# Reordering the first batch of a block-sorted attention and its following projections: two-bank tiles for two v mixes, and two pairs' scores in one session

## The chip, the cores and the metric

The kernel runs on one core of a Trainium2 chip. The time is device microseconds (us) of one execution, and a quoted time is a median of several. A profile is one execution's trace. Its *span* runs from the first to the last recorded instruction and is about 2 us shorter than the time. Engines: PE is TensorE, PEld its weight load, DVE VectorE, ACT ScalarE, POOL GpSimd, SP the queue that issues transfers and DMA transposes.

## The reference, cut to what matters

```python
for _ in range(5):                         # P: softmax, then column normalisation, of sort_net
    P = softmax(P); P = P / P.sum(-2)
k_sorted = einsum('bhij,bhjcd->bhicd', P, k_b)   # "mix" of k over 8 blocks of 96 rows
v_sorted = einsum('bhij,bhjcd->bhicd', P, v_b)   # "mix" of v
attn = softmax(scale * q_b @ k_sorted.T)         # per block, 96 x 96
x = (attn @ v_sorted)                            # 4 batches x 768 tokens, 8 heads x 64 -> 512
out = ((x @ w_a) * (x @ w_b)) @ w_out            # 512 -> 1536 -> 512
```

Two heads make a pair; a batch has four. Attention of batch 0 is done in two halves of four blocks, so that projections of its first half can start while the second half's attention goes on. Batch 0's halves are the changed code.

## The kernel before

The buffers in PSUM, and the helpers:

```python
psA = tile_pool(bufs=2, space=PSUM)     # tiles [128, 2, 512] fp32: two banks each
psF = tile_pool(bufs=4, space=PSUM)     # tiles [128, 512] fp32: one bank each

def mix_first(g, what, engines, fill=0, cols=512):   # 12 matmuls, two copies out
    mix = [psF.tile([P, 512], FP32, tag="F") for _ in range(2)]
    keep_busy(mix[0], fill, cols)                    # dummy matmuls
    mix_mms(g, what, lambda c: mix[c // 3][:, c % 3 * P:(c % 3 + 1) * P])
    for u, eng in enumerate(engines):
        copy(eng, turned(g, what, u), mix[u] ...)    # to kT / vT of pair g

def half_scores(h, hp):   # 8 matmuls into a psA tile, ACT exponential -> eT
def half_v(hp):           # 4 transposes of vT into a psF tile, DVE copy -> vs
def second_v(hp):         # the second half's v: a DMA transpose of vT -> vs
def half_o(h, hp):        # 8 matmuls eT x vs into psA; DVE reciprocal and multiply -> xph
def half_x(h, hp, eng):   # 4 transposes of xph into psF, copy by eng -> xT
def partial(n, *kcs):     # projection matmuls of chunks kcs, begun before the last xT chunk
                          # n < 3: psF tile, n = 3, 4: a psA tile ("two")
# ... cut: order of the first half (see the diff)
# ... cut: ffn_ab(b, m, t): 4 w_a and 4 w_b matmuls, ACT copy a_sb, DVE product hT
def c_(g):                # later pairs: turn q, mix k and v, then
    ...
    if g > HP: return_v(g)                           # DMA transpose vT -> vs, by SP
    if g >= 2 * HP - 2:
        nc.gpsimd.tensor_copy(out=gate, in_=kTs[g % HP][0:1, 0:1])
        load_later(g)                                # load pair g + 2, by POOL
```

The queues of PE, POOL and SP, and in the changed part of ACT and DVE too, run in the program's order. The kernel text sets no semaphores; the waits are added when it is built.

The softmax here doesn't subtract the row's maximum and nothing guards it: scores larger than these inputs give would overflow.

## Time and profile before

| what | before |
|---|---|
| time, median of 3 (range) | 241.52 us (241.12 to 241.68) |
| span of the profile | 239.3 us |
| first mix starts | 13.02 us |
| first scores of the second half start | 25.80 us |
| first unit of batch 1 (its q transposes) starts | 42.28 us |

I call the stretches between the last three rows the first half (12.78 us) and the second half (16.48 us), and what follows the tail (197.02 us). The page and the lines that carry the reading are in the prediction below.

### The profile page before, as it was taken

The page shows a single profiled execution, that of the slowest core. Times are in us where ns is not written, and L with a number is a line of the kernel's source. Part 1 is how long each engine was busy: PE and PEld are TensorE (multiplying, and loading weights), DVE is VectorE, ACT ScalarE, POOL GpSimd, SP SyncE. Part 2 cuts the span into 40 slices and gives each one's busy share as a digit, 9 for nine tenths or more (in the row PEclk, how much of TensorE's full clock was granted, in tenths as well). Part 3 has the DMA queues.
Part 4 walks back from the last instruction along what each step waited for, and adds up shares of the span by engine and source line. Part 5 has one row for each costly group of instructions (what it writes and reads, how often), then busy time and mean ns, then how long its engine had stood idle before and what let it go on. Part 6 is the DMA issues. An engine that isn't in the chain of part 4 may idle for free.

```text
span 239.3 us, 5178 instructions
## 1 busy us (share of the span) xinstructions
PE 233.4 (98%) x2075; PEld 138.7 (58%) x2075; DVE 109.6 (46%) x258; ACT 100.7 (42%) x187; POOL 70.4 (29%) x97
## 2 busy tenths in 40 slices
PE   7999999999999999999999999999999999999994
PEld 7776566666644556666554455666545566655442
DVE  6788467546444234466416243644543244434110
ACT  3675652674530266644630366355500234333001
POOL 8777348773400055072520508211000000000000
PEclk9999999999999999999999999999999999999999
DMA  5999999999998489679996899970434300000132
GB/s 76 203 198 195 161 191 201 201 201 190 176 171 201 111 138 161 109 121 190 139 196 128 181 133 176 171 144 20 77 79 123 130 1 3 0 0 3 56 119 88
DMA packets 65703, 30.88 MB, mean 129 GB/s; under 512 B 42512, under 2 KB 62736, under 8 KB 65680
## 3 DMA queue, kind: packets, MB, share of 16 engines
q0 software_dynamic: 20944, 14.16, 42.7%
q1 hardware_dynamic: 44592, 16.33, 35.3%
q8 instruction: 16, 0.26, 0.4%
q10 hardware_dynamic: 144, 0.07, 0.1%
q14 instruction: 7, 0.06, 0.1%
HBM read 28.32 MB, written 6.29 MB: 145 GB/s over the span
## 4 chain that ended last, share of the span: by engine, by line
PE 95%; DVE 3%; ACT 1%; issue 0%; DVEq 0%
PE pf L360 52%; PE po L405 24%; PE o_ps L236 3%; PE sc L330 2%; PE heat L167 2%; PE mix L175 2%; PE mix L301 2%; PE mixf L175 1%; PE po L390 1%; PE sc L197 1%; PE xt_ps L227 1%; PE q_ps L265 1%; PE two L360 1%; DVE xp L242 1%; PE vs_ps L213 0%; DVE o_sb L163 0%
## 5 line engine op out<-in xcount | busy, mean ns | idle before, releaser
L381 DVE TENSOR_TENSOR hT<-a_sb,pf 128x384 bf16<-128x384 bf16 x95 | 52.6, 554 | 72.2 <-PE pf L360 46.7
L360 PE MATMUL pf<-xT,w_a_sb 128*128 128x384 bf16 x380 | 78.0, 326 | 0.0
L360 PE MATMUL pf<-xT,w_b_sb 128*128 128x384 bf16 x380 | 77.4, 326 | 0.0
L380 ACT CAST a_sb<-pf 128x384 bf16<-128x384 f32 x95 | 45.4, 479 | 61.8 <-PE pf L360 37.7
L405 PE MATMUL po<-w_out_sb,hT 128*128 128x512 bf16 x276 | 61.9, 379 | 0.0
L360 PEld LDWEIGHTS <-w_b_sb 128*128 128x128 bf16 x384 | 37.5, 98 | 24.7
L360 PEld LDWEIGHTS <-w_a_sb 128*128 128x128 bf16 x384 | 35.2, 98 | 22.7
L405 PEld LDWEIGHTS <-hT 128*128 128x128 bf16 x276 | 26.4, 98 | 30.1
L161 ACT COPY o_sb<-po 128x512 f32<-128x512 f32 (+1 forms) x13 | 7.5, 578 | 48.9 <-PE po L405 47.5
L163 DVE COPY o_sb<-po 128x512 f32<-128x512 f32 (+1 forms) x12 | 7.9, 658 | 38.7 <-PE po L405 34.1
L335 ACT ACTIVATE eT<-sc 96x768 bf16<-96x768 f32 x24 | 18.1, 803 | 5.2 <-PE sc L330 5.2
L242 DVE TENSOR_TENSOR xp<-o_ps,rec 96x512 bf16<-96x512 f32 x24 | 15.9, 684 | 0.3
L317 POOL COPY kT<-turned 128x768 bf16<-128x768 bf16 x6 | 5.0, 831 | 32.5 <-DMA turned<-nat 32.5
L96 POOL DMA_DIRECT2D k<-in_k_dram x16 | 11.6, 724 | 4.9 <-DMA w_a_sb<-in_moe_w_a_dram 1.9
L96 POOL DMA_DIRECT2D v<-in_v_dram x16 | 11.5, 722 | 3.6 <-DMA w_b_sb<-in_moe_w_b_dram 2.4
L236 PEld LDWEIGHTS <-eT 96*128 96x128 bf16 x256 | 10.2, 97 | 3.6 <-DVE xp L242 0.6
L236 PE MATMUL o_ps<-vs,eT 96*128 96x65 bf16 x256 | 11.4, 193 | 0.4 <-DVE vs L214 0.2
L96 POOL DMA_DIRECT2D q<-in_q_dram x12 | 8.7, 723 | 3.5 <-DMA w_a_sb<-in_moe_w_a_dram 2.6
L251 POOL COPY qc<-q 128x768 bf16<-128x768 bf16 x10 | 8.4, 844 | 3.9 <-DMA q<-in_q_dram 3.9
L161 ACT CAST nat<-mix 128x768 bf16<-128x768 f32 (+1 forms) x12 | 7.7, 639 | 4.2 <-PE mix L301 2.5
L167 PE MATMUL heat<-warm 128*128 128x128 bf16 x84 | 8.0, 273 | 1.3 <-DVE warm L77 1.3
L585 POOL COPY gate<-kT 1x1 bf16<-1x1 bf16 x4 | 0.7, 178 | 27.1 <-ACT kT L283 22.6
(86 smaller groups left out, 160.4 us busy)
## 6 DMA issues: line engine op xcount, KB each, us to landing
out_dram<-o_sb SPq DMA_DIRECT2D x17, 256.0 KB, 2.0
k<-in_k_dram POOLq DMA_DIRECT2D x16, 192.0 KB, 5.9
v<-in_v_dram POOLq DMA_DIRECT2D x16, 192.0 KB, 6.6
q<-in_q_dram POOLq DMA_DIRECT2D x12, 192.0 KB, 6.8
w_a_sb<-in_moe_w_a_dram POOLq DMA_DIRECT2D x6, 256.0 KB, 10.1
w_b_sb<-in_moe_w_b_dram POOLq DMA_DIRECT2D x6, 256.0 KB, 11.0
w_out_sb<-in_moe_w_out_dram POOLq DMA_DIRECT2D x3, 512.0 KB, 11.2
out_dram<-o_sb SPq DMA_DIRECT2D x12, 128.0 KB, 2.4
```

The source lines that it names most:

```text
L96: nc.gpsimd.dma_start(out=to, in_=_ap(t, base, [[W, P], [S * D, 2], [1, W]]))
L161: nc.scalar.copy(out=out, in_=in_)
L163: nc.vector.tensor_copy(out=out, in_=in_)
L167: nc.tensor.matmul(ps[:, 0:cols], lhsT=warm[:, 0:P], rhs=warm[:, 0:cols], start=True, stop=True)
L236: nc.tensor.matmul(o_ps[:, e, i * (D + 1):(i + 1) * (D + 1)], lhsT=eT[:, hf, e, i * BLK:i * BLK + P], rhs=vs[0:BLK, i0 + i, V0 - 1 + e * ( ...
L242: nc.vector.tensor_tensor(out=_ap(xp, i0 * 2 * D, [[nxp * 2 * D, BLK], [D, 2], [2 * D, NBH], [1, D]]), in0=_ap(o_ps, 1, [[1024, BLK], [511 ...
L251: nc.gpsimd.tensor_copy(out=qc.rearrange("p c e d -> p e c d"), in_=loaded[g][2].rearrange("p e (c d) -> p e c d", c=NCH))
L335: nc.scalar.activation(out=eT[:, hf, :, 0:HB], in_=sc[0:BLK, :, 0:HB], func=AF.Exp, scale=float(scale))
L360: nc.tensor.matmul(pf[:, 0:HW], lhsT=w_sb[:, kc, m * P:(m + 1) * P], rhs=x_cols(b, kc, t), start=(kc == 0), stop=(kc == KA - 1))
L380: nc.scalar.copy(out=a_sb, in_=pf[:, 0:HW])
L381: nc.vector.tensor_mul(out=hT[:, m, t * HW:(t + 1) * HW], in0=a_sb, in1=ab[1][:, 0:HW])
L405: nc.tensor.matmul(held["po"], lhsT=hTs[b][:, m, c * P:(c + 1) * P], rhs=w_out_sb[:, m, :], start=(m == 0), stop=(m == KO - 1))
```

## The change

Its intent is to take waits and session switches out of TensorE's queue in batch 0. The first half gets a searched order, with the v mixes of pairs 0 and 2 in two-bank tiles to free one-bank buffers. In the second half, scores of two pairs follow each other in one session.

```diff
+    def mix_first(g, what, engines, wide=False, fill=0):
+        if wide:
+            both = psA.tile([P, 2, 512], FP32, tag="A", name="mixa")
+            mix = [both[:, 0], both[:, 1]]
+        else: ...
-            mix_first(0, "v", ("act", "dve"), 2, 256)
-            mix_first(0, "k", ("dve", "act"))
-            mix_first(1, "v", ("act", "dve"), 1)
-            mix_first(1, "k", ("act", "dve"))
+            mix_first(0, "k", ("act", "dve"), fill=2)
+            mix_first(0, "v", ("act", "dve"), wide=True)
+            mix_first(1, "k", ("dve", "act"))
+            mix_first(1, "v", ("act", "dve"))
             half_scores(0, 0)
             half_v(0)
-            mix_first(2, "v", ("act", "dve"))
+            mix_first(2, "v", ("dve", "act"), wide=True)
             mix_first(2, "k", ("act", "act"))
             half_o(0, 0)
+            half_v(1)
             half_scores(0, 1)
-            half_v(1)
             half_v(2)
 # ... cut: xT copies of pairs 0, 2, 3 to ACT and of pair 1 to DVE; half_scores(0, 3), half_v(3) earlier;
 # ... cut: mix_first(3, "k") with its two engines swapped; partial order 0, 2, 1, 0, 3, 4 (was 0, 4, 2, 0, 3, 1)
-            # second half: S0 | S1 | O0 S2 | X0 | O1 S3 | X1 | O2 | X2 O3 | X3
+            # second half: S0 S1 | O0 | O1 X0 | S2 S3 | X1 | O2 | O3 X2 | X3
```

The last two lines sum up the new unit list and its counts: S is half_scores, O half_o, X half_x, and a bar is one projection step or more.

More of the change, by code (lines that the diff above doesn't have):

```diff
@@ L176, in mix_mms @@
                                  rhs=s_all[:, 2 * g + e], start=True, stop=True)
-    def mix_first(g, what, engines, fill=0, cols=512):
-        mix = [psF.tile([P, 512], FP32, tag="F", name="mixf") for _ in range(2)]
-        keep_busy(mix[0], fill, cols)
+    def mix_first(g, what, engines, wide=False, fill=0):
+        if wide:
+            both = psA.tile([P, 2, 512], FP32, tag="A", name="mixa")
+            mix = [both[:, 0], both[:, 1]]
+        else:
+            mix = [psF.tile([P, 512], FP32, tag="F", name="mixf") for _ in range(2)]
+        keep_busy(mix[0], fill, 256)
         mix_mms(g, what, lambda c: mix[c // 3][:, c % 3 * P:(c % 3 + 1) * P])
@@ L183, in mix_first @@
             copy(eng, turned(g, what, u),
-                 _ap(mix[u], 0, [[512, P], [P, 3], [CG, NB], [1, CG]]))
+                 _ap(mix[u], 0, [[1024 if wide else 512, P], [P, 3], [CG, NB], [1, CG]]))
     def turned(g, what, u):
@@ L500, in partial @@
                 ab_mms(begun[n], (w_a_sb, w_b_sb)[n % 2], 0, n // 2, 0, kcs)
-            mix_first(0, "v", ("act", "dve"), 2, 256)
-            mix_first(0, "k", ("dve", "act"))
-            mix_first(1, "v", ("act", "dve"), 1)
-            mix_first(1, "k", ("act", "dve"))
+            mix_first(0, "k", ("act", "dve"), fill=2)
+            mix_first(0, "v", ("act", "dve"), wide=True)
+            mix_first(1, "k", ("dve", "act"))
+            mix_first(1, "v", ("act", "dve"))
             half_scores(0, 0)
             half_v(0)
-            mix_first(2, "v", ("act", "dve"))
+            mix_first(2, "v", ("dve", "act"), wide=True)
             mix_first(2, "k", ("act", "act"))
             half_o(0, 0)
+            half_v(1)
             half_scores(0, 1)
-            half_v(1)
             half_v(2)
-            mix_first(3, "k", ("dve", "act"))
+            mix_first(3, "k", ("act", "dve"))
             half_scores(0, 2)
@@ L518 @@
             mix_first(3, "v", ("act", "act"))
-            half_x(0, 0, "dve")
+            half_x(0, 0, "act")
             half_o(0, 2)
             second_v(1)
-            half_x(0, 1, "act")
             half_scores(0, 3)
+            half_x(0, 1, "dve")
+            half_v(3)
+            half_x(0, 2, "act")
             partial(0, 0)
-            half_v(3)
             partial(0, 1)
-            half_x(0, 2, "dve")
             half_o(0, 3)
             second_v(2)
-            partial(4, 0, 1, 2)
-            partial(2, 0, 1, 2)
-            partial(0, 2)
-            half_x(0, 3, "dve")
-            partial(3, 0, 1, 2)
-            partial(1, 0, 1, 2)
+            partial(2, 0, 1, 2)
+            partial(1, 0, 1, 2)
+            partial(0, 2)
+            half_x(0, 3, "act")
+            partial(3, 0, 1, 2)
+            partial(4, 0, 1, 2)
             begun = [begun[n] for n in range(5)]
@@ L557, in O, with S, X @@
                     second_v(HP - 1)
-            us = [lambda: half_scores(1, 0)]
-            for hp in range(HP):
-                if hp + 1 < HP:
-                    us.append(lambda hp=hp: half_scores(1, hp + 1))
-                if hp > 0:
-                    us.append(lambda hp=hp: half_x(1, hp - 1, "dve"))
-                us.append(lambda hp=hp: O(hp))
-            us.append(lambda: half_x(1, HP - 1, "dve"))
-            return us
+            def S(hp):
+                half_scores(1, hp)
+                half_scores(1, hp + 1)
+            def X(hp):
+                half_x(1, hp, "dve")
+            return [lambda: S(0), lambda: O(0), lambda: O(1), lambda: X(0), lambda: S(2),
+                    lambda: X(1), lambda: O(2), lambda: O(3), lambda: X(2), lambda: X(3)]
         def c_(g):
@@ L657 @@
         steps += [lambda m=m: ffn_ab(0, m, 0) for m in range(3, KO)]
-        interleave(steps, units_half(), (0, 0, 1, 1, 2, 1, 2, 1, 1, 2, 1, 0))
+        interleave(steps, units_half(), (0, 0, 1, 0, 1, 2, 1, 1, 1, 2, 1, 0))
         for b in range(B):
```

## The prediction

> **What bounds the kernel now.** I read the page first, then the chain of work that ended last in order of time, then the timeline from 12 us to 48 us engine by engine, and last the DMA issues of POOL over the same stretch.
>
> ```profile
> PE 233.4 (98%) x2075; PEld 138.7 (58%) x2075; DVE 109.6 (46%) x258; ACT 100.7 (42%) x187; POOL 70.4 (29%) x97
> PE 95%; DVE 3%; ACT 1%; issue 0%; DVEq 0%
> ```
>
> The chain is TensorE for 95% of the span; the DVE 3% is mostly the normalisation loop before 12 us, which the diff doesn't touch. So a microsecond counts only if it leaves TensorE's queue, either as work, as a switch between kinds of work, or as a wait. The 98% cannot be taken as useful time: waits hide in it. The changed code occupies 13.0 us (first mix) to 42.3 us (first unit of batch 1). Everything before is untouched and everything after should only shift.
>
> In the first half (13.0 to 24.1 us) the visible losses are few:
>
> ```profile
> 13.02 0.53 PE L175 MATMUL mixf<-s_all,v 128*64 128x128 bf16 x12 [0.19 <-DVE s_all L153]
> 13.35 0.53 PE L175 MATMUL mixf<-s_all,k 128*64 128x128 bf16 x12
> 13.94 0.38 PE L167 MATMUL mixf<-warm 128*128 128x512 bf16 x1
> 14.25 0.53 PE L175 MATMUL mixf<-s_all,v 128*64 128x128 bf16 x12
> ...
> 21.55 0.42 PE L236 MATMUL o_ps<-vs,eT 96*128 96x65 bf16 x8 [0.18 <-DVE vs L214]
> ```
>
> Read starts, not durations: each group's printed end overlaps the next start. The third mix starts at 14.25, not at about 13.7, because all four one-bank buffers are taken by the first two mixes and a dummy matmul of 512 columns sits in the gap. The last half_o of the phase starts at 21.55 although the transpose before it started at 21.03 and such a group takes about 0.25: it waits about 0.27 us for DVE's copy of v (21.07 + 0.42) and ScalarE's exponential (20.68 + 0.81 = 21.49). Both helpers are nearly without gaps before that. That makes the phase a three-engine race, not a TensorE one.
>
> In the second half (24.1 to 42.3 us) the chain shows what a session of scores costs between projection matmuls:
>
> ```profile
> 25.80 0.35 PE sc L197 x8
> 26.14 1.41 PE pf L360 x8
> 27.55 0.28 PE sc L197 x8
> 27.82 1.41 PE pf L360 x8
> 29.23 0.25 PE o_ps L236 x8
> 29.48 0.28 PE sc L197 x8
> 29.75 1.41 PE pf L360 x8
> 31.16 0.17 PE xt_ps L227 x4
> 31.33 1.30 PE pf L360 x8
> ...
> 59.46 0.45 PE sc L330 x16
> 59.90 1.41 PE pf L360 x8
> ```
>
> Eight projection matmuls take 1.30 us after an output or a transpose session, 1.41 beside a score session: the switch costs 0.11 us on top of 0.28 us of score work, some 0.38 a session (0.35 to 0.38 by starts). One session of 16, as later batches have it, costs 0.45 + 0.11 = 0.56.
>
> **What the skill says.** The Trainium skill, "TensorEngine Tiling (Array Packing)", section Tiling Modes, Key Properties: changing the tiling mode drains TensorE. The trace agrees: scores are 64*128 tiles between 128*128 matmuls, and they show the extra 0.11 us. Outputs and transposes (96*128) show none, so I charge nothing for moving those. "Perfetto Trace Analysis", section Per-engine timelines: a TensorE end time is modelled. Hence I use starts. "PSUM — Partial Sum Buffer", Terms: a bank is 2 KiB per partition and there are eight; the trace's program uses four one-bank and two two-bank buffers, all eight, so a mix in a two-bank tile relieves one pool only by loading the other. No run here shows the collision the same entry warns of.
>
> **The change, part by part.** The first half keeps the same mixes, scores, outputs and partial projections. It drops the 512-column dummy (0.31 us by starts, 13.94 to 14.25), puts k before v, mixes v of pairs 0 and 2 in two-bank tiles, and gives two of the transposed-output copies net to ScalarE. I walked the new order by hand, queue by queue, with durations from the rows (mix 0.33 to 0.45, scores 0.28, half_v 0.32, half_o 0.25 to 0.35, transposes 0.17 to 0.27, ScalarE copy 0.39 to 0.48, exponential 0.71 to 0.81, DVE copy 0.48 to 0.55, reciprocal and multiply 0.92, DVE copies of half_v and xT about 0.4 and 0.3). This is an estimate.
>
> - The four first mixes go out 13.02, 13.37, 13.70, 14.03. The fourth waits a little for the first one's copies (14.14) and ends near 14.4; before it ended at 15.04. That is 0.6 us ahead.
> - The first half_v then needs a one-bank buffer, and with rotation it gets the one DVE empties third: 13.58 + 2 x 0.48 + 0.55 = 15.09. So it starts near 15.1 instead of 15.32: two thirds of the lead is lost at once.
> - First half_o 16.2 (was 16.52), second scores 16.87 (was 16.87; it needs the two-bank tile of the v mix, free at about 16.5, and comes after half_v(1)), second half_o 18.2 (was 18.43), third 19.27 (was 19.51; needs the third exponential, 18.35 + 0.81), fourth scores 19.66 (was 20.20; they now come before a transpose).
> - The last exponential ends near 21.0 instead of 21.49, because ScalarE copies one xT first. DVE copies xT(1) before half_v(3): 20.0 + 0.69 for the third multiply, then 0.3, then 0.42, ends near 21.3. The last half_o starts near 21.36, 0.19 ahead. Three partial sessions fill the wait for its multiply, so the first closing projection matmul starts near 23.9 instead of 24.14. **First half: minus 0.24 us.**
>
> Second half. Four score sessions become two. By the numbers above each merge saves 2 x 0.375 - 0.56 = 0.19 us, 0.38 in all. But the first merged session pays a new wait. The two-bank buffers go round in turn; with partial(4) now after partial(3), the first scores inherit the buffer of partial 3, emptied by the second DVE product of the projections, no longer the one emptied by a ScalarE copy at 25.75. Before, that product ended at 26.03, which is 1.89 us after the first closing matmul at 24.14. TensorE, with nine matmuls of 0.163 us, is ready 1.56 us after it. The wait is 1.94 - 1.56 = 0.38 against 0.10 us before, 0.28 more. Against that, two waits of transposes for the DVE multiply (starts 37.59 and 39.40, some 0.17 and 0.08 us later than a normal follow-on) should go, since an output session or a projection step now stands between: 0.25. **Second half: 0.38 - 0.28 + 0.25 = minus 0.35 us.**
>
> Sum: 0.24 + 0.35 = 0.59 us, 241.52 - 0.59 = 240.93, rounded to 240.9.
>
> **Rivals.** First, weight arrival becomes the wall. POOL's issues show when earlier loads landed, since it stalls for them:
>
> ```profile
> 31.54 0.71 POOL L96 DMA_DIRECT2D k<-in_k_dram  x1 [1.37 <-DMA w_b_sb<-in_moe_w_b_dram]
> 31.82 0.81 PE L360 MATMUL pf<-xT,w_b_sb 128*128 128x384 bf16 x4
> ```
>
> Counting issues and landings in order, that load is the fourth w_b chunk, and the matmuls that use it start 0.28 us later. In my walk these now start at 31.82 - 0.24 + 0.09 (first merge less its wait) - 0.37 + 0.25 (one score session later, one output session earlier) = 31.55, just at the landing. So if the first half gains more than I think, the surplus is taken here: this caps the total near 0.6 us, unless the loads land earlier too. For: DMA moves some 200 GB/s without pause here. Against: transposes by DMA share the engines, and may shift.
>
> Second, the helpers give back all of the first half: if DVE or ScalarE runs as late as before at the last half_o, the gain there is 0, and the total 0.35, 241.2 us. For: both are almost always busy between 13.4 and 21.5. Against: before, ScalarE has gaps of 0.26 and 0.19 us, DVE of 0.21, 0.21 and 0.24, which an order can close; with all closed the last half_o could start near 20.8, a gain of 0.7 us, 240.4 without the weight wall.
>
> Third, the merged sessions stall ScalarE: two exponentials in a row (1.5 us) delay the next projection copy by about 0.65 us and could hold TensorE for a one-bank buffer. The later batches do just that at 51.33 and TensorE shows no wait, so I give it little: 241.5 at worst.
>
> **Range and chances.** The span of the three old runs is 0.56 us, as large as the effect. I add that to a step error of some 0.3 us either way: 240.2 to 241.7. A 2% move is 4.8 us, a fifth of everything between 13 and 42 us that isn't projection work plus more; nothing in the diff adds or removes that. Faster 0.01, within 0.98, slower 0.01.
>
> **What would show it right or wrong.** In the changed trace: fourth mix over by 14.4; last half_o near 21.36; first closing projection matmul near 23.9; first scores of the second half held for a DVE product; two score sessions of 16 at 0.45 us; no wait for xph in the last two transposes; first unit of batch 1 at about 41.7 instead of 42.27, and from there the same distance to the end. The number is wrong if w_b arrives later and TensorE waits for DMA, if buffers don't rotate as assumed, or if a later stage absorbs the shift.

## The result, and the profile after

| | before | after |
|---|---|---|
| time, median of 6 | 241.56 us (240.93 to 242.09) | 240.64 us (240.58 to 240.69, and one slow run of 247.53) |
| ratio of fast runs | | 0.9965, 95% interval 0.9947 to 0.9982 |
| span of the profile | 239.3 us | 238.8 us |
| time less span, profiled run | 241.44 - 239.3 = 2.1 us | 240.58 - 238.8 = 1.8 us |
| first mix starts | 13.02 us | 12.66 us |
| first half | 12.78 us | 13.07 us |
| second half | 16.48 us | 16.01 us |
| tail | 197.02 us | 197.06 us |

A ratio here is the mean time of one kernel's fast runs over that of the other's fast runs of the same rounds, so it isn't quite the ratio of the medians. The small gain is clear of the noise in these runs, and the time falls inside the predicted range. But the table already says that one of the two halves went the wrong way.

The page of the changed kernel, busy time by engine and the chain by engine:

```profile
PE 232.2 (97%) x2074; PEld 138.1 (58%) x2074; DVE 108.9 (46%) x256; ACT 101.4 (42%) x189; POOL 70.4 (29%) x97
PE 92%; DVE 5%; ACT 1%; DMA 1%; issue 1%; DVEq 0%
```

TensorE has 3 points less of the chain and DVE 2 more. Only part of that is the first half, where the path runs through copies of DVE and ACT from 13.55 to 16.86 us and before ran through TensorE almost alone. The rest is the start, no part of the change: up to 5.0 us the path of this profile runs through a load and the normalisation loop, that of the profile before through dummy matmuls. TensorE's timeline of the changed kernel's first half:

```profile
13.66 0.53 PE L175 MATMUL mixf<-s_all,v 128*64 128x128 bf16 x12
14.12 0.34 PE L201 MATMUL sc<-qT,kT 64*128 64x96 bf16 x8
14.68 0.40 PE L217 MATMUL vs_ps<-ident,vT 128*128 128x128 bf16 x4 [0.21 <-DVE vT L163]
...
16.18 0.39 PE L217 MATMUL vs_ps<-ident,vT 128*128 128x128 bf16 x4
16.91 0.35 PE L201 MATMUL sc<-qT,kT 64*128 64x96 bf16 x8 [0.34 <-ACT vT L161]
...
21.49 0.41 PE L240 MATMUL o_ps<-vs,eT 96*128 96x65 bf16 x8
```

The four first mixes come as close together as hoped: the fourth starts 1.00 us after the first, at 13.66. The trouble is the second scores at 16.91. They need a two-bank tile, and it was held by the v mix of pair 2 until ACT had copied it. That group starts 4.25 us after the first mix, against 3.85 in the old order (16.87 - 13.02). So a lead of 0.6 us at the fourth mix (14.61 - 13.02 = 1.59 us before, 1.00 now) has become a lag of 0.40 us. The two lines of before:

```profile
14.61 0.50 PE L175 MATMUL mixf<-s_all,k 128*64 128x128 bf16 x12
16.87 0.34 PE L197 MATMUL sc<-qT,kT 64*128 64x96 bf16 x8
```

Why ACT was late is in its own timeline and in DVE's of the changed kernel:

```profile
15.80 0.55 DVE L163 CAST vT<-mixa 128x384 bf16<-128x384 f32 x1
```

```profile
14.67 0.83 ACT L206 ACTIVATE eT<-sc 96x768 bf16<-96x768 f32 x1
16.38 0.48 ACT L161 CAST vT<-mixa 128x384 bf16<-128x384 f32 x1 [0.88 <-DVE vT L163]
```

DVE copies one bank of the tile from 15.80 to 16.35. ACT, idle since about 15.5, starts on the other bank only at 16.38, 0.03 us after DVE is done. The two banks are different, yet the copies run one after the other. The trace puts ACT's idle time down to DVE's copy, which had ended just before; copies out of two one-bank tiles overlap (v2_narrow, below). The mix of pair 0 shows the same thing turned round: ACT at 13.55, DVE at 14.06 rather than beside it.

TensorE's timeline of the second half, the same kernel:

```profile
25.73 0.64 PE L201 MATMUL sc<-qT,kT 64*128 64x96 bf16 x16
26.30 0.82 PE L364 MATMUL pf<-xT,w_a_sb 128*128 128x384 bf16 x4
...
32.27 0.51 PE L201 MATMUL sc<-qT,kT 64*128 64x96 bf16 x16
32.72 0.82 PE L364 MATMUL pf<-xT,w_a_sb 128*128 128x384 bf16 x4
```

There are now two score sessions of 16. By starts, the second costs 0.45 us, as in the later batches. The first takes 0.57: its second pair waits for the buffer that DVE's second product empties (that product ends at 25.97). Eight projection matmuls after a session still take 1.41 us. So the merge took out two switches, and the second half is 0.47 us shorter.

### The profile page after: what moved, and what is told of

Same layout as the page of the kernel before. It is cut to its first block, busy times and chain, and to the rows that moved or that the text cites. A ratio compares the mean times of both kernels' runs of the same rounds, so it can differ in the third digit from the quotient of the medians.

```text
span 238.8 us, 5175 instructions
## 1 busy us (share of the span) xinstructions
PE 232.2 (97%) x2074; PEld 138.1 (58%) x2074; DVE 108.9 (46%) x256; ACT 101.4 (42%) x189; POOL 70.4 (29%) x97
## 4 chain that ended last, share of the span: by engine, by line
PE 92%; DVE 5%; ACT 1%; DMA 1%; issue 1%; DVEq 0%
PE pf L364 52%; PE po L409 25%; PE o_ps L240 3%; PE sc L334 2%; PE mix L175 2%; PE mix L305 2%; PE po L394 1%; PE sc L201 1%; DMA p_nat<-in_sort_net_dram 1%; PE xt_ps L231 1%; DVE vT L163 1%; PE mixf L175 1%; PE heat L167 1%; PE q_ps L269 1%; PE two L364 1%; DVE xp L246 1%
## 5 line engine op out<-in xcount | busy, mean ns | idle before, releaser
L96 POOL DMA_DIRECT2D k<-in_k_dram x16 | 11.6, 724 | 5.0 <-DMA w_a_sb<-in_moe_w_a_dram 2.0
L240 PEld LDWEIGHTS <-eT 96*128 96x128 bf16 x256 | 10.4, 97 | 3.8 <-DVE xp L246 0.6
## 6 DMA issues: line engine op xcount, KB each, us to landing
w_a_sb<-in_moe_w_a_dram POOLq DMA_DIRECT2D x6, 256.0 KB, 10.4
```

The source lines that it names most:

```text
L96: nc.gpsimd.dma_start(out=to, in_=_ap(t, base, [[W, P], [S * D, 2], [1, W]]))
L240: nc.tensor.matmul(o_ps[:, e, i * (D + 1):(i + 1) * (D + 1)], lhsT=eT[:, hf, e, i * BLK:i * BLK + P], rhs=vs[0:BLK, i0 + i, V0 - 1 + e * ( ...
```

## The experiments

Twelve runs in three sessions, each session on another chip, each kernel beside before on its own chip. "First half" is always the distance from the first mix to the first scores of the second half.

### Which half, and why: second_only, first_only, v2_narrow, before_again

**second_only** is before with the new unit list and counts alone:

```diff
 # before, first half untouched
-            us = [S0 | S1 | O0 S2 | X0 | O1 S3 | X1 | O2 | X2 O3 | X3]
+            us = [S0 S1 | O0 | O1 X0 | S2 S3 | X1 | O2 | O3 X2 | X3]
```

> The kernel before with only the second half's new order (scores of two pairs in one session). Theory A (the gain is the second half's, the first half's new order gives nothing or loses): first closing projection matmul 11.1 us after the first mix as before, second half (from there to the first q transposes of batch 1) about 17.7 us against 18.13 before, time 0.4 to 0.6 us under before, so ratio about 0.998. Rival B (both halves gain): ratio about 0.9985, and the changed kernel clearly faster than this one by 0.3 us or more.

Measured: first half 12.78 us, second half 16.04 us, both as theory A says. The time was not: 243.68 us median, ratio 1.0068 (1.0036 to 1.01), with four fast runs from 241.87 to 243.98 and two slow ones (246.52 and 251.16, clock 0.984 and 0.978). The profile, of a fast run, shows where it went. TensorE's timeline of second_only:

```profile
69.25 1.46 PE L405 MATMUL po<-w_out_sb,hT 128*128 128x512 bf16 x6
72.78 0.65 PE L236 MATMUL o_ps<-vs,eT 96*128 96x65 bf16 x16 [2.07 <-DMA vs<-vT]
```

TensorE stood 2.07 us for the DMA transpose of pair 7's v. And here are busy times and TensorE's granted clock in stretches of 2 us of the same run (after the engines come PEclk, DMA share, GB/s):

```profile
72.00:74.00 2.00, 1.22 (x20) 0.90 (x21) 0.75 (x2) 0.00 (x0) 0.00 (x0) 1.00 1.10 282
74.00:76.00 2.00, 1.78 (x6) 0.73 (x6) 0.95 (x3) 0.59 (x1) 0.00 (x0) 0.52 0.75 215
76.00:78.00 2.00, 2.00 (x7) 0.68 (x7) 0.00 (x0) 0.00 (x0) 0.00 (x0) 0.63 0.73 145
78.00:80.00 2.00, 2.00 (x11) 0.94 (x10) 0.69 (x1) 0.00 (x0) 0.00 (x0) 1.00 0.36 84
```

The wait costs twice: after it the granted clock is 0.52, then 0.63, for some 4 us, and full only by 78 us. The tail is 200.65 us instead of 197.0, so 3.6 us are lost to a wait of 2.07. The lost clock of the two stretches, 2 x 0.48 + 2 x 0.37 = 1.7 us by estimate, accounts for the rest. On this chip, a faster second half alone made the kernel slower. That was no part of theory A or of rival B.

**first_only** is the changed kernel with the old unit list and counts.

> The changed kernel with the second half's old order. Theory A: first closing matmul 11.4 us after the first mix (0.3 us later than before), second half 18.0 to 18.2 us, time equal to before or up to 0.3 us over: ratio 1.000 to 1.0015. Rival B: ratio 0.998 or 0.9985.

Measured: 241.19 us, ratio 1.0013 (0.9979 to 1.0047), fast runs 240.85 to 241.22 apart from the profiled one of 243.23, and one slow run of 246.83. Second half 16.49 us, so the old length. The profiled run is a poor sample for the first half: TensorE waited in it for loads of v (0.3 and 0.9 us), and the first half took 14.35 us. It also waited 0.92 us for the transpose of pair 7's v, until 74.07 us, with no fall of the clock after it, and its tail is 197.81 us. So this run supports theory A by its time and second half only; the rest of the evidence has to come from the next one.

**v2_narrow** is the changed kernel with one word out:

```diff
-            mix_first(2, "v", ("dve", "act"), wide=True)
+            mix_first(2, "v", ("dve", "act"))
```

> The changed kernel with the v mix of pair 2 back in two one-bank tiles. Theory A says the two copies out of one two-bank tile run one after the other (DVE 15.80 to 16.35, then ScalarE 16.38 to 16.86) and hold the second scores until 16.91. Then here both copies overlap, the second scores start 0.3 to 0.5 us earlier after the first mix (4.25 us now, about 3.85 then), and the first closing matmul comes about 11.0 to 11.2 us after the first mix in place of 11.4. Rival: one-bank buffers run short instead (v2 waits for the copies of k1 and v1) and the phase is as long or longer.

Measured: first half 12.74 us, 0.33 less than the changed kernel. The copies overlap again, as ACT's and DVE's timelines of v2_narrow show:

```profile
15.91 0.48 ACT L161 CAST vT<-mixf 128x384 bf16<-128x384 f32 x1
```

```profile
16.13 0.54 DVE L163 CAST vT<-mixf 128x384 bf16<-128x384 f32 x1
```

The second scores start 4.15 us after the first mix (4.25 in the changed kernel); that is less than expected, since k of pair 2 now waits for a one-bank buffer (the rival's point), and the rest is won behind it, as ACT is free earlier. The edit also frees a two-bank buffer, so the 0.33 us is what the order of the copies and the buffer that they hold cost together; no run here separates the two. The time: fast runs 240.56, 240.58 and 241.37, ratio 0.9987 (0.996 to 1.0013), but three of six runs slow (244.8 to 246.3, clock 0.985 to 0.992). Theory A's account of the first half holds in the trace.

**before_again**, a second profile of before:

> The kernel before, unchanged, for a second profile. Theory: the first mix started at 13.02 us in the one profile of before and at 12.66 in that of the changed kernel though no instruction ahead of it differs; that is scatter of the start, so this profile may show either, while first mix to first closing matmul stays at 11.1 us and the second half at 18.1 us. Rival: 13.0 again, which would tie the start to the program.

Measured: 241.68 us for one run, state unknown; first mix at 13.25 us, first half 12.78, second half 16.48, tail 197.09. Over all 14 profiles the first mix starts anywhere from 12.42 to 13.25 us, with either first half. The 0.36 us that the changed kernel's profile gained before the first mix is scatter.

### A wall of transfers: second_delay, second_gate, v2_gate, after_again

**second_delay** adds work to second_only:

```diff
-            mix_first(1, "v", ("act", "dve"), 1)
+            mix_first(1, "v", ("act", "dve"), 3)      # two more dummy matmuls
```

> The kernel with only the second half's new order, plus two more dummy matmuls of 512 columns on TensorE ahead of the third mix, some 0.43 us of pure delay. Theory C (a wall of transfers: that kernel lost time because TensorE, about 1 us ahead, reached the last outputs of batch 0's second half before the transposed v of pair 7 had landed, waited 2.07 us at 70.7 us and then ran several us at a lower granted clock): the added delay removes most or all of the wait, and the kernel with MORE work is faster: fast runs about 240.6 to 241.2 against 241.9 to 244.0 without. Rival D (the long runs were chance, or a fault of the new order itself): 0.4 us slower than without, 242 to 244.

Measured: first half 13.22 us (0.44 longer), tail 197.08, no wait for the transpose, all six runs fast, 240.80 to 241.53, ratio 1.0008 (0.9994 to 1.0022). More work, and steadily faster than second_only. The chips differ, which is why second_only was run once more below.

**second_gate** and **v2_gate** change what the next load waits for, in second_only and in v2_narrow:

```diff
-  nc.gpsimd.tensor_copy(out=gate, in_=kTs[g % HP][0:1, 0:1])
+  nc.gpsimd.tensor_copy(out=gate, in_=vss[g % NBUF][0:1, 0, V0:V0 + 1] if g == 2 * HP - 1
+                        else kTs[g % HP][0:1, 0:1])
```

> The kernel with only the second half's new order, with the load of the pair after pair 8 held until the transposed v of pair 7 has landed (it was held only for pair 7's k copy[...]). Theory C: the transpose lands earlier, no wait for it at 70.7 us, and with the start scatter of 12.4 to 13.2 us the fast runs are 240.2 to 241.0, the new order's 0.46 us at last visible against before (ratio about 0.998). Rival D: no change, 242 to 244.

Measured for second_gate: first half 12.78, second half 16.01 us, and no wait for the transpose in its profile though TensorE came to the outputs at 70.51 us, when second_only's TensorE had to wait. Fast runs 240.81 to 241.29, ratio 1.0006 (0.9991 to 1.0022), so the expected 0.998 was missed, and two of six runs were slow (244.0 and 244.9 us of span). So the hold doesn't remove every loss. The tail of its profile is 0.44 us longer than v2_gate's (197.49 to 197.05); most of that is a wait of 0.34 us, ending at 93.67 us, for a later DMA transpose, of q.

> The changed kernel with pair 2's v mix back in one-bank tiles and the same hold on the load. Theory C: 0.33 us shorter in the first half than the changed kernel, and without the risk of running into the late transpose: fast runs 239.9 to 240.6, ratio 0.997, no slow runs at a clock of 0.99. Rival D: 240.6 at best, slow runs as often as before (3 of 6).

Measured for v2_gate: 240.36 us, all five runs fast, 240.20 to 240.58, ratio 0.9974 (0.9961 to 0.9986). First half 12.74, second 16.01, tail 197.05. POOL's timeline of v2_gate bounds the landing time of the transpose, since POOL waits for it:

```profile
69.60 0.18 POOL L589 COPY gate<-vs 1x1 bf16<-1x1 bf16 x1 [12.12 <-DMA vs<-vT]
```

The transpose had landed by 69.6 us, 1.25 us before the outputs that read it (70.85). Without the hold, second_only's reached TensorE at 72.78. This is the best version and faster than before. That its fast runs beat those of the changed kernel isn't shown: on the same chip two of the latter took 240.40 us (next run); what it has ahead is that none of its five runs was slow, against three of six.

> The changed kernel once more, on this chip, against the same runs of before. Theory: first mix to first scores of the second half 13.07 us, from there to the first q transposes 16.0 us, the end 197.05 us after those, as in its first profile; 240.6 us, ratio 0.9965 to 0.999, about 1.75 us of time outside the span against 2.1 for before. Rival: the ratio of the first session was that chip's and here the two are equal.

Measured for after_again: first half 13.08, second half 16.01, tail 197.02 us, as in the first session. Fast runs 240.40, 240.40 and 241.36, ratio 0.9987 (0.9965 to 1.0009), and three of six runs slow (246.2 to 250.9, clock 0.985 to 0.993), where two of eleven of before were slow. On this chip, then, the change itself isn't clearly faster. Its profile is at the edge: the last outputs are one group at 70.98 us, right after the projections, with no wait shown.

One reading of the traces tells what the wall is. A DMA view of a window with nothing but this transpose's issue gives its time from issue to landing, here of second_only and of v2_narrow:

```profile
vs<-vT SPq DMA_TRANSPOSE x1, 10.4
vs<-vT SPq DMA_TRANSPOSE x1, 5.2
```

| profiles | issued at, us | issue to landing, us | wait of TensorE, us |
|---|---|---|---|
| second_only, second_again, both_narrow | 62.22, 62.38, 62.02 | 10.4, 11.6, 11.8 | 2.07, 3.21, 3.45 |
| first_only | 64.65 | 9.3 | 0.92 |
| before, before_again, before_xact, second_delay | 63.24 to 63.48 | 5.0, 8.2, 5.0, 5.4 | none |
| after, after_again, v2_narrow | 62.54 to 62.71 | 6.2, 8.3, 5.2 | none |
| with the hold: second_gate, v2_gate, after_gate | 62.18 to 62.60 | 7.3, 6.9, 4.3 | none |

In all 14 profiles TensorE is ready for the outputs 8.3 us after the issue, since the issue moves ahead with TensorE. So, other than theory C has it, a lead by itself doesn't use up any slack: the profiles that show a wait are those whose transpose takes clearly over 8.3 us. In those four it lands within about 0.2 us of the q load issued just after it, in the other profiles without the hold 1.5 us or more before that load. The earliest issues without the hold took longest, and second_gate's, as early but with the load held back, took 7.3 us; that speaks for the load as the cause. But before_again's 8.2 us shows the old kernel near the edge too, and why first_only's late issue was slow as well stays open.

### Controls: after_gate, second_again, both_narrow, before_xact

> The changed kernel with only the hold on the load (the pair after pair 8 waits until the transposed v of pair 7 has landed). Theory C (its slow runs, 3 of 6 on the last chip, come from TensorE running into that late transpose): fast runs 240.2 to 240.6 as without the hold, no or one slow run in six. Rival D (slow runs are the chip's own): two to three slow runs again. First half 13.07 us to the first scores of the second half, as without the hold.

Measured for after_gate (the changed kernel with the hold): 240.53 us, none of six runs slow (240.34 to 241.81), ratio 0.998 (0.9963 to 0.9997), first half 13.07. Three slow runs against none in six fits theory C, but the chips differ and no slow run of the changed kernel was profiled, so I don't call their cause shown.

> The kernel with only the second half's new order once more, on another chip than its first session, since the delayed and the held version ran on another chip than it did. Theory C: fast runs again scattered from 240.8 to 244 with slow ones among them, above before on the same chip (ratio 1.002 to 1.007). Rival D: 240.8 to 241.3 and as steady as before, which would make the first session's loss that chip's.

Measured for second_again: two fast runs, 240.58 and 240.95, ratio of those 0.9981, and four of six runs slow (244.56 to 246.85), while all eleven of before on this chip lie between 240.91 and 241.67. The expected ratio above 1 was missed, because here the lost runs are classed as slow. The profiled run, a slow one, has TensorE waiting 3.2 us for the same transpose. The unsteadiness came back on a second chip, so it isn't one chip's.

**both_narrow** is the changed kernel without any two-bank mix.

> The changed kernel with neither v mix in a two-bank tile: what the two-bank tile is worth for pair 0. With pair 0's v in a two-bank tile alone the first scores of the second half come 12.74 us after the first mix. Theory: without it the third mix waits for the first copies as in before (0.3 to 0.5 us), but the copies of v of pair 0 overlap (no 0.29 us hold on DVE), so 12.6 to 13.0. Rival: the two-bank tile is what the new order lives from, and this takes 13.2 us or more.

Measured: first half 12.58 us, the shortest of all, 0.49 below the changed kernel. So in the first half the two-bank tiles cost, both of them, and the new order is better without. But the time of this single run was 244.52 us, state unknown. TensorE's and its weight loads' timelines of both_narrow:

```profile
73.96 1.04 PE L240 MATMUL o_ps<-vs,eT 96*128 96x65 bf16 x16 [3.45 <-DMA vs<-vT]
```

```profile
30.80 0.47 PEld L364 LDWEIGHTS <-w_b_sb 128*128 128x128 bf16 x4 [0.18 <-DMA w_b_sb<-in_moe_w_b_dram]
```

It ran into the wall: 3.45 us, and a tail of 201.6. The second line is the weight arrival that the prediction named: at 30.8 us, earlier than in any other profile, the weight load sat 0.18 us for w_b. In second_only, at 31.02 us, it sat 0.24 us; that fits a second half of 16.04 us there in place of 16.01.

> The kernel before with three of the first half's transposed-output copies on ScalarE and one on DVE, as in the changed kernel (it was one and three): a look at the time outside the span, 2.1 us for all kernels with the old first half and 1.75 with the new one. If the instruction counts of ScalarE and DVE set it, this shows 1.75. If it is 2.1, something else in the first half does, and that stays open. First half within 0.2 us of 12.78.

Measured for before_xact (before with its xT copies moved between ACT and DVE as in the change): 242.15 us for one run, span 240.4, state unknown, so 1.75 us outside the span, as expected if the two engines' instruction counts set it. The span itself holds a wait of 0.71 us, ending at 95.35 us, for the transpose of q that second_gate waited for, so the time says nothing of what the moved copies are worth. First half 12.91 us, 0.13 longer. All kernels with ACT's 189 and DVE's 256 instructions have about 1.75 to 1.8 us outside the span, all with 187 and 258 about 2.1. What happens there isn't recorded, so the mechanism stays open.

## Why the prediction was right or wrong

The time, 240.64 us for 240.9 predicted, is right, and partly by luck. Of the 0.59 us that the two halves were to give, they gave 0.18; a term outside both, which the prediction didn't have, made up for most of the rest. The sign "first unit of batch 1 at about 41.7" came true (41.74) only because this profile's first mix came 0.36 us earlier.

- **Second half, predicted minus 0.35, measured minus 0.47.** The merge of sessions is as predicted. Sized wrong was the new wait ahead of the first merged session: 0.38 us was claimed, "the first scores inherit the buffer of partial 3". They started 1.66 us after the first closing matmul in both kernels (24.07 to 25.73, and 24.14 to 25.80). The start follows ACT's copy of partial 4 (25.18 + 0.50 = 25.68 us), not DVE's product, so the buffers don't go round in turn as I assumed. Only the session's second pair waited for the product, 0.12 us. Of the two transpose waits that were to go (0.25), the later one kept about 0.1 us: pair 3's transposes start 0.26 us after the matmul ahead of them (38.61 to 38.87), as a normal follow-on would 0.16. These terms sum to 0.38 - 0.12 + 0.15 = 0.41 us; the last 0.06 I haven't placed.
- **First half, predicted minus 0.24, measured plus 0.29.** The step that failed is the walk's "it needs the two-bank tile of the v mix, free at about 16.5". On the profile of before's clock (0.36 us later) it came free at 17.2 (16.86 + 0.36). I had let ACT and DVE empty a two-bank tile side by side; then it would have been free when DVE was done, at 16.7 (16.35 + 0.36). The other 0.5 us is ACT's copy, which waited for DVE's. v2_narrow shows what the tile of pair 2 cost, 0.33 us, and both_narrow both tiles, 0.49, of the 0.53 us between prediction and measurement. A smaller slip: the walk's own terms for DVE before the last half_o, 20.0 + 0.69 + 0.3 + 0.42, give 21.4, not "near 21.3". The old profile held the answer, in later batches' v mixes, which use such tiles. DVE, then ACT, of before:

```profile
49.65 0.56 DVE L163 CAST vT<-mix 128x384 bf16<-128x384 f32 x1
```

```profile
50.24 0.48 ACT L161 CAST vT<-mix 128x384 bf16<-128x384 f32 x1
```

ACT begins 0.03 us after DVE ends. There it costs TensorE nothing, which is why I passed over it.

- **What made up for it** lies outside both halves. Time outside the span fell by 0.35 us with the first half's new order, a term that the prediction didn't have. 0.47 - 0.29 + 0.35 = 0.53 us is the repeatable gain; after_gate on its chip had 0.2% of 241 us, about 0.5. The first session's ratio (0.35%, about 0.84 us) is 0.3 us more. Luck of the start, which in the two profiles was 0.36 us, would explain that, but the starts of the other runs aren't known.
- **The first rival, weights as a wall**, named the right kind of limit at the wrong place. Its landing time was read a little late, too. Two lines of the changed kernel, POOL's and TensorE's, show the matmuls on that chunk begin before POOL gets its go:

```profile
31.60 0.71 POOL L96 DMA_DIRECT2D k<-in_k_dram  x1 [1.38 <-DMA w_b_sb<-in_moe_w_b_dram]
```

```profile
31.52 0.81 PE L364 MATMUL pf<-xT,w_b_sb 128*128 128x384 bf16 x4
```

  The w_b chunk was late by little (0.18 us in both_narrow's weight loads, 0.24 in second_only's) and never cost much. The transfer that bites is the DMA transpose of pair 7's v at 70 us: from 40 to 72 us the DMA engines of before move 190 GB/s on average with short pauses, and the transpose took 5.0 us in some profiles and 9.3 to 11.8 in others, against 8.3 us until it is needed. The prediction wrote of transposes that they "may shift" and assumed everything after 42.3 us would only shift; second_only disproves that. That the changed kernel's slower first half spared it most of this is argued from both_narrow, whose faster one met the wall in its single run.
- **The second rival** (helpers give all of the first half back) was nearer the truth than my main line, by another mechanism. **The third** (two exponentials in a row hold TensorE) did not happen: no wait stands in the second half beyond those named.

On the skill: the page "PSUM — Partial Sum Buffer", section PSUM bank collisions raise a hardware error, says that two engines on different banks run clean. By that page the chip would have allowed what I assumed. The trace shows only that one copy waits for the other; that the wait comes from the build and not from the chip isn't shown, as no run here tried the copies without it. The page "TensorE: Matmul & The Clock Gate", section What's actually happening, says that the array falls to half its clock after an idle window of about 3.4 us and recovers after a busy one. The 0.52 after the wait in second_only and the full clock some 4 us later agree with the two states; the length of the wait, 2.07 us, doesn't agree with the window (see the last section). The page "DMA: Bandwidth & Descriptors", section Queues, rings and completion order, says that each DMA engine takes turns between the queues that have work. Shorter transposes with the load held back would agree with that, and with the hold they took 4.3 to 7.3 us, without it 5.0 to 11.8; the ranges overlap, so three profiles on two chips don't show it.

## What to carry to other kernels

Before moving a result into a larger buffer, look in the trace how such buffers are emptied elsewhere: if two engines take turns on it, the buffer is held for the sum of both copies. Measure a reordering by distances between milestones rather than by the total, and run its parts alone: here one half gained, one lost, and the total hid both. When a kernel's busiest engine gets ahead, ask which transfer it meets next, and look at how much that transfer's own time scatters (5.0 to 11.8 us here) and not at one profile's. A wait of 2 us cost 3.6, and with one load held back that wasn't urgent no profile had that wait.

## What the Trainium skill lacked or had wrong

- "PSUM — Partial Sum Buffer" says that different banks can be read at once, but doesn't mention that two engines' copies out of one two-bank tile may still run one after the other: ACT began 0.03 us after DVE's end, having stood idle for 0.88 us.
- "TensorE: Matmul & The Clock Gate" asks for an idle window of about 3.4 us; here a wait that the trace puts at 2.07 us was enough for a granted clock of 0.52, and the price was 3.6 us in all. A wait of 0.92 us (first_only) brought no fall.
- "TensorEngine Tiling (Array Packing)" gives no figure for the drain at a change of mode: here 0.11 us per score session between 128*128 matmuls, none for 96*128 ones.
- No page that I looked at ties the time outside the span to the program: it was about 2.1 us, and 1.75 us with two instructions moved from DVE to ACT.
- No page that I looked at gives the time of a DMA transpose beside loads: 5.0 to 11.8 us from issue to landing.
